# 29 products of zeros in place of 23 ahead of the first transposes

## The chip, the cores and the metric

The kernel runs on one core of one Trainium2 chip. The metric is device time in microseconds (us) of one execution. The kernel before has a median of 334.01 us over three executions (333.19 to 335.12). Engines are named as the profile names them: PE (TensorE, matrix products; PEld its weight loads), DVE (VectorE), ACT (ScalarE), POOL (GpSimd) and SP (SyncE, here a queue for transfers).

## The reference

Two layers follow each other. The first is attention with a band of 32 positions to either side and 8 global positions, for 8 batches of 8 heads, 576 positions and 64 dimensions. The second takes the 4608 tokens of 512 values through two dense products with a softplus between them.

```
mask = |pos_i - pos_j| <= 32, or i global, or j global
attn = softmax(where(mask, q @ k.T / 8, -1e9));  x = attn @ v
out  = softplus(x @ w_in) @ w_out        # 512 -> 2048 -> 512
```

## The kernel before, in words

The attention is done in blocks of 32 queries. A group of four blocks (a pair n in the code) has its scores s of 8 heads in two PSUM banks; a score product has a form of 32x128, one block of queries against four blocks of keys (previous, own, next, global). DVE takes row maxima m, ACT the exponentials st, DVE or POOL normalises them to pn, DVE transposes them to pt, and PE multiplies by v into xo. For the first two batches q and k are turned on PE: transposes tr against an identity, and beside them small products pick that choose the global rows. The output xo is cast to xT, and the dense layer follows in eight or nine phases: products h (xT by w_in, L1288), softplus to g on ACT, products o (g by w_out, L1299).

The first four groups have the mask added on PE, by a product of the identity with a mask tile (s, L1062 and L1072). L1062 waits for the mask tile, which DVE writes last in L641. The value products of the first phase are opened ahead by four products of zeros into xo (L1239), one for each of its PSUM banks; the real ones are L1253.

The order of the instructions on every engine is made before the run by a planner (class `_Order`). It goes through a fixed table of jobs (`ORDER`) and gives each job a planned time, from costs per operation in nanoseconds and a model of when PE's instructions arrive in blocks of 256. Each tile of PSUM gets, in that planned time, the bank that comes free first.

Where the planner sees PE without work for at least 700 ns in the first 34,000 ns (`WARM`), `keep` puts in a group of products of zeros: `fill_in` multiplies a cleared part of a spare v tile (vb) by itself, 128x128 by 128x512, into a free bank (tile warm, L731). Nothing reads the results. Before, their number is the planned gap times `FILL` (0.55) over `FILLT` (220 ns), rounded down. The first gap starts at PE's planned start of 1200 ns and ends at the planned start of L1062. Each group is also counted in the model of instruction blocks (`self.issued`), and takes a bank from then on.

Of the kernel before, what the change touches and what calls it, by code (L numbers as in the profile page):

```python
# [20 lines left out]
class _Order:  # L21
# [131 lines left out]

    WARM = 0
    FILL, FILLT, NARROW, NFILL, NFILLT = 0.55, 220, 0, 0.8, 140
    STARVE = 900
    fill = None

    def keep(self, t0, t1, order):

        if self.fill is None or t1 > self.WARM or t1 - t0 < 700:
            return
        free = [(self.closed(k), n) for n, k in enumerate(self.banks)]
        free = [x for x in free if x[0] is not None and x[0] <= t0 + 300]
        if not free:
            return
        n = min(free)[1]
        thin = t0 < self.NARROW
        share, step = (self.NFILL, self.NFILLT) if thin else (self.FILL, self.FILLT)
        count = int((t1 - t0) * share / step)  # L170
        key = ("warm", len(order))
        j = dict(cost={"PE": (0, 0)}, emit=lambda e: self.fill(key, count, thin), at=t0, end=t0 + count * step, on="PE", n=-1, deps=[])
        self.fetch = self.stall(t0, count * step, 2 * count)[1]
        self.issued += 2 * count
        self.users[key] = [j]
        self.banks[n] = key
        self.bank[key] = n
        order.append(j)
# [26 lines left out]
    def run(self, free):  # L205
# [16 lines left out]
        while ready:  # L222
# [6 lines left out]
            for j in self.picked(ready):  # L229
# [6 lines left out]
                for e in j["cost"] if not self.given else [self.given[0][1]]:  # L236
# [7 lines left out]
                    elif e == "DVE" and j["port"]:  # L244
                        if self.other[0] <= t + 100 and self.other[1] > t:
                            t = self.other[1] + self.STARVE
                    elif e == "POOL" and t < self.mine[1]:
                        t = self.mine[1] + (self.STARVE if t < self.mine[0] else 0)
                    if self.TABLE and j["table"] and j["table"] != table:
# [1222 lines left out]
```

## Time and profile before

| what | value |
|---|---|
| median of three executions | 334.01 us (333.19 to 335.12) |
| profiled execution | 333.27 us, of which 331.2 us are the span from the first to the last instruction |
| mean granted TensorE clock | 0.979 |
| products of zeros (warm, L731) | 41, busy 13.9 us |
| products h and o | 768, busy 138.2 us, and 592, busy 138.3 us |

The page divides the span by engine; the chain of waits follows the end of the program back to what released each step; the timeline lists instructions in order of time, with the idle time before them in brackets and what ended it. Views by stretch give the busy time of each engine and the clock that was granted to TensorE, as a share of full speed. A span shorter than the time of the execution is normal: some microseconds lie before the first and after the last instruction.

### The profile page before, as it was taken

Reading aid. Unit: us, or ns where it says so; the run is one execution under the profiler, and the core shown is the slowest. Engines: PE = TensorE matmul, PEld = TensorE weight load, DVE = VectorE, ACT = ScalarE, POOL = GpSimd, SP = SyncE. Lnnn points to the kernel's source line nnn. Section 1 sums busy time; section 2 is a strip of 40 time slices with the busy share of each in tenths; the row PEclk is TensorE's granted clock in tenths of the full one; section 3 lists DMA queues with packets and bytes.
Section 4 is the critical chain, followed back from the end, with each engine's and each line's share of the span. In section 5 each row is a group of like instructions: output and inputs, shape, how many; then the busy total and the mean of one; then the engine's idle time right before and its main releaser. Section 6 shows DMA issues by size and latency. Waiting matters only on the chain.

```text
span 331.2 us, 12091 instructions
## 1 busy us (share of the span) xinstructions
PE 322.2 (97%) x5285; PEld 172.5 (52%) x5285; DVE 220.2 (66%) x386; ACT 234.1 (71%) x459; POOL 196.0 (59%) x175
## 2 busy tenths in 40 slices
PE   8797999999999999999999999999999999999996
PEld 3455886565555445544455445444544454454444
DVE  7587588856997799894895985278785970431000
ACT  5579879686698896388648867996749746915622
POOL 7825908996786568859579396829183927240000
PEclk9767999999999999999999999999999999999999
DMA  7997898989898999999989980370010011001002
GB/s 193 187 204 187 186 185 144 150 141 212 174 162 147 175 215 143 202 206 200 181 164 185 152 189 2 115 158 3 4 65 0 36 65 70 27 34 63 34 32 96
DMA packets 168796, 42.14 MB, mean 127 GB/s; under 512 B 153256, under 2 KB 165800, under 8 KB 168744
## 3 DMA queue, kind: packets, MB, share of 16 engines
q1 hardware_dynamic: 155928, 27.15, 46.3%
q0 software_dynamic: 10944, 11.08, 16.5%
q10 hardware_dynamic: 1872, 3.15, 2.5%
q8 instruction: 41, 0.67, 0.9%
q14 instruction: 11, 0.09, 0.1%
HBM read 36.71 MB, written 9.44 MB: 139 GB/s over the span
## 4 chain that ended last, share of the span: by engine, by line
PE 92%; DVE 3%; ACT 2%; DMA 1%; issue 1%; DVEq 0%
PE o L1299 38%; PE h L1288 38%; PE xo L1253 5%; PE s L1079 4%; PE ov L999 2%; PE tr L859 1%; PE pick L888 1%; PE warm L731 1%; DMA gi<-in_global_idx_dram 1%; ACT st L1115 1%; PE sg L970 1%; PE pick L901 1%; PE s L1062 0%; DVE qx L722 0%; ACT qx L722 0%
## 5 line engine op out<-in xcount | busy, mean ns | idle before, releaser
L1299 PE MATMUL o<-wout,g 128*128 128x512 bf16 (+1 forms) x592 | 138.3, 374 | 0.0
L1288 PE MATMUL h<-xT,win 128*128 128x512 bf16 (+3 forms) x768 | 138.2, 328 | 0.0
L1294 ACT ACTIVATE g<-h 128x512 bf16<-128x512 f32 (+3 forms) x192 | 84.5, 504 | 29.9 <-PE h L1288 26.7
L1134 POOL TENSOR_TENSOR pn<-st,rs 128x1024 bf16<-128x1024 f32 (+1 forms) x38 | 66.9, 1769 | 58.1 <-DVE rs L1128 52.9
L1288 PEld LDWEIGHTS <-win 128*128 128x128 bf16 x768 | 67.6, 99 | 59.8 <-issue 1.1
L1299 PEld LDWEIGHTS <-g 128*128 128x128 bf16 x592 | 55.9, 98 | 60.7 <-ACT g L1294 1.0
L1102 POOL TENSOR_TENSOR st<-st,m 128x1024 f32<-128x1024 f32 x32 | 60.2, 1893 | 27.7 <-DVE m L1096 27.7
L1083 DVE TENSOR_TENSOR st<-s,mask 128x512 f32<-128x512 f32 x64 | 41.1, 676 | 18.5 <-PE s L1079 18.4
L1126 DVE TENSOR_REDUCE sm<-st 128x8 f32<-128x1024 f32 x32 | 38.5, 1203 | 14.9 <-ACT st L1119 14.7
L1096 DVE TENSOR_REDUCE m<-st 128x8 f32<-128x1024 f32 x32 | 37.9, 1208 | 0.3
L722 ACT COPY osb<-o 128x512 f32<-128x512 f32 (+1 forms) x30 | 17.2, 577 | 22.6 <-PE o L1299 20.2
L1119 ACT ACTIVATE st<-st 128x1024 f32<-128x1024 f32 x32 | 32.7, 1053 | 0.3
L1143 DVE STREAM_TRANSPOSE pt<-pn 128x512 int32<-128x512 int32 x36 | 24.5, 689 | 5.2 <-POOL pn L1134 5.1
L722 ACT CAST xT<-xo 128x512 bf16<-128x512 f32 (+3 forms) x28 | 11.7, 467 | 18.4 <-PE xo L1253 18.4
L722 DVE CAST xT<-xo 128x512 bf16<-128x512 f32 (+3 forms) x20 | 11.3, 600 | 18.6 <-PE xo L1253 18.6
L1294 ACT ACT_TABLE_LOAD x15 | 19.2, 1283 | 1.7 <-PE h L1288 1.5
L1119 ACT ACT_TABLE_LOAD x14 | 18.0, 1283 | 0.7 <-ACT osb L722 0.4
L719 POOL TENSOR_SCALAR qb<-stage 128x1152 bf16<-128x1152 f32 (+2 forms) x15 | 16.8, 1126 | 1.7 <-DMA stage<-in_q_dram 1.1
L1079 PEld LDWEIGHTS <-qx 64*32 64x32 bf16 x1152 | 10.4, 92 | 9.5 <-issue 6.3
L722 POOL CAST vb<-stage 128x1152 bf16<-128x1152 f32 x12 | 13.7, 1145 | 2.7 <-DMA stage<-in_v_dram 2.7
L731 PE MATMUL warm<-vb 128*128 128x512 bf16 x41 | 13.9, 485 | 1.3 <-DVE vb L553 1.3
L1079 PE MATMUL s<-kx,qx 64*32 64x128 bf16 x1152 | 14.6, 225 | 0.2
(127 smaller groups left out, 291.4 us busy)
## 6 DMA issues: line engine op xcount, KB each, us to landing
stage<-in_v_dram SPq DMA_DIRECT2D x56, 144.0 KB, 4.3
stage<-in_q_dram SPq DMA_DIRECT2D x48, 144.0 KB, 3.9
stage<-in_k_dram SPq DMA_DIRECT2D x48, 144.0 KB, 4.3
out_dram<-osb POOLq DMA_DIRECT2D x24, 256.0 KB, 3.2
out_dram<-osb ACTq DMA_DIRECT2D x11, 256.0 KB, 2.0
stage<-in_q_dram SPq DMA_DIRECT2D x4, 512.0 KB, 5.9
stage<-in_k_dram SPq DMA_DIRECT2D x4, 512.0 KB, 7.1
win<-in_moe_w_in_dram POOLq DMA_DIRECT2D x8, 256.0 KB, 7.4
```

The lines of the kernel that those rows point to most:

```text
L722: {"ACT": nc.scalar.copy, "DVE": V.tensor_copy, "POOL": nc.gpsimd.tensor_copy}[e](out, in_)
L1079: nc.tensor.matmul(out=PS["s", n, g][quad(a), x, :], lhsT=qx[b % 2][rows(g), a, j * BL:(j + 1) * BL], rhs=kx[b % 2][rows(g), a, e0 * BL:(e ...
L1083: V.tensor_tensor(out=PS["st", n][:, h, :, :], in0=PS["s", n, h][:, :, :], in1=mask[:, h, j0:j0 + PB, :, :].rearrange("p j s i -> p j (s i ...
L1096: V.reduce_max(out=m[:], in_=flat(PS["st", n], h0, h1), axis=AX)
L1102: on(e).tensor_tensor(out=t, in0=t, in1=over(PS["m", n, y][:], SL * BL), op=OP.subtract)
L1119: nc.scalar.activation(out=t, in_=t, func=AF.Exp)
L1126: V.reduce_sum(out=sm[:], in_=flat(PS["st", n], h0, h1), axis=AX)
L1134: on(e).tensor_tensor(out=PS["pn", n][:, :, :, h0:h1].rearrange("p x s h -> p h x s"), in0=PS["st", n][:, h0:h1], in1=PS["rs", n, y][:].re ...
L1143: V.transpose(out=bass.AP(base.tensor, base.offset, ap=[list(base.ap[0]), [2 * STEP, PB // 2], [STEP + BL // 2, 2], [1, SL * BL]]), in_=PS ...
L1288: nc.tensor.matmul(out=h[:, :], lhsT=w_in_t[c // 4][:, kd, c % 4 * P:(c % 4 + 1) * P], rhs=PS["xT", m][:, kd, lo:hi], start=(kd == 0), sto ...
L1294: nc.scalar.activation(out=PS["g", m, c][:, lo:hi], in_=PS[key][:, lo_of(c, hi - lo)], func=AF.Softplus)
L1299: nc.tensor.matmul(out=PS["o", m, ns, a][:, :], lhsT=PS["g", m, kf][:, ns * P:(ns + 1) * P], rhs=w_out_t[kf // 4][:, kf % 4, a:z], start=( ...
```

## The change

`keep` counts differently where the gap starts before 5400 ns of planned time (`COLD`). It takes 0.93 of the gap (`LONG`) in place of 0.55, and counts the part ahead of 5400 ns at 427 ns a product (`COLDT`), the rest at 220 ns. Only the first group starts that early. All other costs, the table of jobs and the other groups' rule stay.

```
+    COLD, COLDT, LONG = 5400, 427, 0.93
...
         share, step = (self.NFILL, self.NFILLT) if thin else (self.FILL, self.FILLT)
         count = int((t1 - t0) * share / step)
+        if t0 < self.COLD:
+            span = (t1 - t0) * self.LONG
+            cold = min(span, self.COLD - t0)
+            count = int(cold / self.COLDT + (span - cold) / step)
+            step = span / count
```

The order on DVE, ACT, POOL and SP is the same as before. On PE three places differ. The new code is six lines longer, so a line above 172 of before has a number higher by six after (L1062 is L1068, L1079 is L1085, L1239 is L1245, L1253 is L1259, L1288 is L1294, L731 is L737).

The first place is the end of the first group, ahead of the mask product. Rows of before (46 to 53):

```order
L731 MATMUL warm<-vb_67 128x512
L1062 LDWEIGHTS ident [waits DVE_49]
L1062 MATMUL s<-mask,ident 128x512 [waits Pool_49]
L1062 LDWEIGHTS ident [waits Activation_49]
L1062 MATMUL s<-mask,ident 128x512 [waits Pool_49]
L859 LDWEIGHTS kb [waits Activation_49]
L859 MATMUL tr<-ident,kb 128x128
```

and of the change (58 to 64):

```order
L737 MATMUL warm<-vb_67 128x512
L1068 LDWEIGHTS ident [waits DVE_49]
L1068 MATMUL s<-mask,ident 128x512 [waits Pool_49]
L1068 LDWEIGHTS ident [waits Activation_49]
L1068 MATMUL s<-mask,ident 128x512 [waits Pool_49]
L865 LDWEIGHTS kb [waits Activation_49]
L865 MATMUL tr<-ident,kb 128x128
```

The group ahead of these rows has 29 products in place of 23, so everything behind stands 12 rows later (a weight load and a product each).

The second place is PE between the last scores of the fourth group and the first value products. A wait names the engine that is waited for. Rows of before (691 to 706):

```order
L1079 LDWEIGHTS qx_68
L1079 MATMUL s<-kx_70,qx_68 32x128
L731 LDWEIGHTS vb_67
L731 MATMUL warm<-vb_67 128x512 [waits Activation_49]
...
L1239 LDWEIGHTS vb_67
L1239 MATMUL xo<-vb_67 128x128 [waits PE_49]
...
L1239 LDWEIGHTS vb_67 [waits DVE_49]
L1239 MATMUL xo<-vb_67 128x128 [waits Activation_49]
L1239 LDWEIGHTS vb_67
L1239 MATMUL xo<-vb_67 128x128 [waits Activation_49]
L1253 LDWEIGHTS vb_66
L1253 MATMUL xo<-pt,vb_66 64x64 [waits DVE_49]
```

and of the change (703 to 714):

```order
L1085 LDWEIGHTS qx_68
L1085 MATMUL s<-kx_70,qx_68 32x128
L1245 LDWEIGHTS vb_67
L1245 MATMUL xo<-vb_67 128x128 [waits Activation_49]
L1245 LDWEIGHTS vb_67
L1245 MATMUL xo<-vb_67 128x128 [waits PE_49]
...
L1245 LDWEIGHTS vb_67 [waits DVE_49]
L1245 MATMUL xo<-vb_67 128x128 [waits Activation_49]
L1259 LDWEIGHTS vb_66
L1259 MATMUL xo<-pt,vb_66 64x64 [waits DVE_49]
```

The two products of zeros are gone. Row 703 was the weight load of the fourth L1239; now it is the weight load of the last score product, and the four L1239 stand at 705 to 712. With that group gone, xo and most later tiles of PSUM (323 of 365) have another bank than before.

The third place is PE behind the first 60 products of h. Rows of before (923 to 932):

```order
L1288 LDWEIGHTS win_127
L1288 MATMUL h<-xT,win_127 128x128
L731 LDWEIGHTS vb_67
L731 MATMUL warm<-vb_67 128x512
L731 LDWEIGHTS vb_67
L731 MATMUL warm<-vb_67 128x512
L731 LDWEIGHTS vb_67
L731 MATMUL warm<-vb_67 128x512
L1253 LDWEIGHTS vg_74
L1253 MATMUL xo<-pt,vg_74 64x256 [waits DVE_49]
```

and of the change (931 to 938):

```order
L1294 LDWEIGHTS win_127
L1294 MATMUL h<-xT,win_127 128x128
L737 LDWEIGHTS vb_67
L737 MATMUL warm<-vb_67 128x512
L737 LDWEIGHTS vb_67
L737 MATMUL warm<-vb_67 128x512
L1259 LDWEIGHTS vg_74
L1259 MATMUL xo<-pt,vg_74 64x256 [waits DVE_49]
```

Three products of zeros have become two. In all PE has 10,578 rows in place of 10,572, and 44 products of zeros in place of 41.

## The prediction

> **What bounds the kernel now.** I read the page's shares first, then the chain of waits, then the start of the timeline, since the change acts there.
>
> ```profile
> span 331.2 us, 12091 instructions
> PE 322.2 (97%) x5285; PEld 172.5 (52%) x5285; DVE 220.2 (66%) x386; ACT 234.1 (71%) x459; POOL 196.0 (59%) x175
> PE 92%; DVE 3%; ACT 2%; DMA 1%; issue 1%; DVEq 0%
> ```
>
> TensorE sets the end: 92% of the chain that ended last is PE. A microsecond won at the start reaches the end only if it lies on that chain. The timeline (start, length, engine, line, count, idle time before it) shows the stretch that the change fills:
>
> ```profile
> 1.26 6.91 PE L731 MATMUL warm<-vb 128*128 128x512 bf16 x23 [1.26 <-DVE vb L553]
> 4.65 0.15 PEld L731 LDWEIGHTS <-vb 128*128 128x128 bf16 x1 [0.28 <-issue]
> 4.99 2.69 PEld L731 LDWEIGHTS <-vb 128*128 128x128 bf16 x13 [0.18 <-issue]
> 10.24 0.60 PE L1062 MATMUL s<-mask,ident 128*128 128x512 bf16 x2 [2.07 <-DVE mask L641]
> ```
>
> The 23 products of zeros run from 1.26 to 8.17; then PE idles for 2.07 us, until VectorE has written the mask that L1062 reads. No product of zeros touches that VectorE work.
>
> The granted clock over stretches of 3.41 us, cut where it steps (columns: stretch, length, PE busy and count, clock, DMA share, GB/s):
>
> ```profile
> 4.88:8.30 3.42, 3.29 (x15) 1.00 1.18 294
> 8.30:11.71 3.41, 1.47 (x26) 1.00 1.53 225
> 11.71:15.12 3.41, 2.94 (x40) 0.50 2.16 147
> 15.12:18.54 3.42, 3.42 (x81) 0.50 1.46 201
> 18.54:21.95 3.41, 3.41 (x51) 0.50 1.22 201
> 21.95:25.36 3.41, 3.41 (x113) 1.00 1.24 205
> 25.36:28.78 3.42, 1.58 (x63) 1.00 0.63 138
> 28.78:32.19 3.41, 3.41 (x70) 0.50 0.98 262
> ```
>
> All steps lie on one grid of 3.41 us. Two stretches with PE busy for under half (1.47 and 1.58 us) are each followed by half clock; a full one of large products (18.54 to 21.95) brings it back. The first products also run at half pace although the column still shows 1.00: single weight loads of 0.15 us up to 4.65, 13 in 2.69 us from 4.99. So the products do their work on the clock only if they make the stretch 8.30 to 11.71 count as busy.
>
> **The change part by part.** The listings show three edits on PE and none on the other engines: 6 products more at the head, 2 fewer before the first value products (L1239), 1 fewer after the first 60 products of h.
>
> *Six more at the head.* At full clock the pitch is (2.69 - 0.10) / 12 = 0.216 us. Six take 6 x 0.216 = 1.29 us of 2.07 idle, so the last ends at 8.17 + 1.29 = 9.46, and 0.78 us of idle is left. Cost 0; cover: the VectorE mask chain. Without cover they would cost 1.29.
>
> *Two fewer before L1239.* First the timeline of that place, then the chain of waits (start, length, what), then the instruction queue (packets, MB, share).
>
> ```profile
> 25.71 0.60 PE L731 MATMUL warm<-vb 128*128 128x512 bf16 x2
> 25.94 0.37 PEld L1239 LDWEIGHTS <-vb 128*128 128x128 bf16 x3
> 28.48 0.10 PEld L1239 LDWEIGHTS <-vb 128*128 128x128 bf16 x1 [2.17 <-issue]
> 27.09 0.40 ACT L1010 ACTIVATE vg<-ov,grs 128x128 bf16<-128x128 f32 x1
> 27.05 0.71 DVE L1143 STREAM_TRANSPOSE pt<-pn 128x512 int32<-128x512 int32 x1
> 27.86 0.66 DVE L1094 TENSOR_REDUCE m<-s 128x4 f32<-128x512 f32 x1
> ```
> ```profile
> 27.28 0.22 PE xo L1239
> 27.50 0.99 issue
> 28.71 0.60 PE xo L1253 x46
> ```
> ```profile
> q8 instruction: 41, 0.67, 0.9%
> ```
>
> The two products end at 26.31 and PE waits anyway until 28.48: their removal saves nothing. But the wait is not a data wait. The fourth L1239 loads its weights only at 28.48, although its data (vg, 27.49) and those of the next rows (pt, 27.76) are there. The instruction queue moved 41 packets for 10,572 PE rows, 258 each; so I take it that row 703, where that load stands, begins a block that had not arrived. The Trainium skill (Runtime: NRT & Kernel Launch, Instruction fetch mechanics) gives 16 KiB blocks of 256 instructions; 0.67 MB in 41 packets agrees. The stall stays at row 703, and the change puts another instruction there: the last pair of scores, then four L1239. Behind the late pair wait four openings of 0.054 us (128 columns, a quarter of the 512-column pitch of 0.216), some 0.2 us. Against it, the row whose issue asks for the block comes 12 rows, six products, earlier: between 0 and 0.43 us (six of the 60 h products, 4.32 us below). Net between -0.2 and +0.2; I take +0.1, since the six rows there are scores, smaller than h's. The row maximum at 27.86 reads the other bank's scores, already written; if it waited for the late pair, it would end near 29.3, where VectorE's next step waits for xo anyway (28.71 + 0.60 = 29.31).
>
> *One fewer after h.* The VectorE row of the timeline, then the chain.
>
> ```profile
> 31.51 1.27 DVE L1143 STREAM_TRANSPOSE pt<-pn 128x512 int32<-128x512 int32 x2
> ```
> ```profile
> 29.32 0.96 PE warm L731 x2
> 30.28 4.32 PE h L1288 x60
> 34.60 0.65 PE warm L731 x3
> 35.25 1.01 PE xo L1253 x75
> ```
>
> Here the products of zeros are on the chain: the tile that xo reads (pt) was there by 32.78 (31.51 + 1.27), yet it starts behind 0.65 us of three zero products. One fewer is -0.22 us. It could be lost again at the next ScalarE wait (0), so between -0.22 and 0; I take -0.2, since the chain stays on PE behind it (xo at 35.25).
>
> *PSUM banks.* With one group of zeros gone, later tiles get other banks. The rows of before cannot show that cost; PE was idle for only 3.1 us after 40 us (291 - 287.89), so it lies between -1 and +1. I take 0: the planner picks banks by the same rule.
>
> ```profile
> 40.00:331.00 291.00, 287.89 (x4678) 150.91 (x4676) 191.03 (x305) 204.96 (x350) 169.18 (x118) 1.00 0.60 119
> ```
>
> *The clock.* In 8.30 to 11.71 PE's busy time becomes 1.47 + (9.46 - 8.30) = 2.63 of 3.41 us, 77%. Is that enough? For: only stretches under 50% were followed by a drop. Against:
>
> ```profile
> 8.30:11.71 3.41, 1.02 (x12) 1.00 1.53 225
> 15.12:18.54 3.42, 1.70 (x23) 0.50 1.46 201
> ```
>
> These are the same stretches for the transposes (tile tr) alone. 15.12 to 18.54 was 100% busy, half of it transposes, and did not lift the clock: they seem to weigh little. Without them the new stretch holds 2.63 - 1.02 = 1.61 us, 47%, hardly more than the 1.58 that lost the clock at 28.78. So I take the clock to drop at 11.71 as before. The Trainium skill (TensorE: Matmul & The Clock Gate, Part 4) says that transposes do not count as PE busy in the same way; the trace agrees, 3.42 us busy at 0.50. Its closing table asks only for no idle gaps over about 3 us; by that the 2.07 us gap would have cost nothing, which the drop at 11.71 contradicts.
>
> *Sum.* 0 + 0.1 - 0.2 + 0 + 0 = -0.1 us. Against the profiled execution's own time (333.27: span 331.2 and 2.07 around it) that is 333.17. That execution lies 0.74 under the median, near the fastest of 333.19 to 335.12; from the median 334.01 I get 333.9.
>
> **The rivals.**
>
> *The clock is kept (faster).* If 77% is enough, the next stretch runs at full clock. The chain's transposes show what it is worth, and a row of ScalarE what could follow:
>
> ```profile
> 10.85 0.22 PE tr L859 x4
> 11.07 0.08 PE pick L865 x4
> 12.89 0.45 PE tr L859 x4
> 13.33 0.09 PE pick L865 x4
> 13.96 0.89 PE warm L731 x2
> ```
> ```profile
> 21.89 1.01 ACT L982 ACTIVATE pg<-sg,gnb 128x320 bf16<-128x320 f32 x2 [1.20 <-DVE gnb L977]
> ```
>
> A set of transposes and picks takes 0.30 at full clock and 0.54 at half; three sets lose 0.7 us, and the two zero products 0.45. Part goes to VectorE's and ScalarE's copies behind them, so I put 0.5 on the chain, -0.1 - 0.5: 333.4. The stretch 11.71 to 15.12 is then itself thin (transposes and 0.43 us of zeros) and would drop the clock at 15.12. Only if it held to 21.95 would the 6.8 us there, all PE, shrink too; then ScalarE's wait of 1.20 goes as well, 1.7 in all: 332.2. Chances 0.20 and 0.06.
>
> *The products overshoot.* The grid of the clock need not start where it did here. If the clock comes up to 3.2 us later, each later microsecond moves the end of the zeros by 1 - 0.216 / 0.43 = 0.50 us (0.43 is the pitch of the single loads, 0.15 + 0.28 idle), at most to 9.46 + 1.6 = 11.06 against 10.24. The last 0.2 us drain while the next runs, which leaves +0.6, where 23 products would still end before 10.24. It decides once the clock comes more than 1.6 us later. Against: this profile has 0.78 to spare. The chain then moves by what is over, -0.1 + 0.6: 334.5. Chance 0.16. The Trainium skill (TensorE: Matmul & The Clock Gate, Part 1) calls the window free-running with a run-variable number of cold products; a single trace cannot show it.
>
> *A second drop (slower).* With two zero products gone, PE's gap of 26.31 to 28.48 begins some 0.5 us earlier. Where the grid cuts this gap in two, before could keep its clock and the change lose it: place 25.71, price up to 3.41 us at half clock in the 60 products of h, 1.7. It decides when one stretch falls under about 1.6 us busy. Here the clock drops there already, so nothing is added: 335.6, chance 0.06.
>
> **How the numbers follow.** No change of the clock has 0.52, kept for one stretch 0.20, overshoot 0.16, kept to 21.95 0.06, second drop 0.06. This measurement tells apart about 0.5%, 1.7 us: the first three lie within it, and only 332.2 and 335.6 sit at its edge. With some room for banks and scatter: faster 0.09, same 0.83, slower 0.08. The likeliest is 333.9; the range takes the kept stretch (333.4), the overshoot (334.5), a microsecond for the banks to either side and the scatter of a median: 332.8 to 335.0.
>
> **What would show it.** The head: one group of 29, L1062 still at about 10.2 with idle of about 0.8; a later start says overshoot. The clock: 0.50 from 11.7 says the six bought nothing; 1.00 until 15.1 says the window counted as busy. The block: a weight load of L1079 alone near 28.4 with idle "issue", L1239 right behind. The h group: two zeros behind it and xo some 0.2 us earlier. I am wrong if the clock stays at 1.00 through 12 to 22, or if idle time after 40 us leaves 3 us by more than one.

## The result and the profile after

The changed kernel has a median of 332.32 us against 334.41 for the kernel before beside it: a ratio of 0.994 (95% interval 0.9914 to 0.9966), 2.1 us or 0.6% faster. The prediction said 333.9, no measurable change, with a range down to 332.8: it was wrong. The profiled execution took 331.25 us, 2.02 under that of before, with a mean clock of 0.995 in place of 0.979.

The page of the changed kernel: span, shares, and the shares of the chain by engine.

```profile
span 329.2 us, 12097 instructions
PE 319.7 (97%) x5288; PEld 171.3 (52%) x5288; DVE 219.3 (67%) x386; ACT 233.9 (71%) x459; POOL 195.9 (60%) x175
PE 91%; DVE 2%; SPq 2%; DMA 2%; issue 1%; ACT 0%
```

PE bounds the kernel as before; its busy time fell by 2.5 us although it does three products more. The timeline shows what happened at the head, at row 703 and behind the first h:

```profile
1.26 8.97 PE L737 MATMUL warm<-vb 128*128 128x512 bf16 x29 [1.26 <-DVE vb L559]
10.27 0.61 PE L1068 MATMUL s<-mask,ident 128*128 128x512 bf16 x2
...
26.42 0.23 PE L1085 MATMUL s<-kx,qx 64*32 64x128 bf16 x1 [3.02 <-issue]
26.58 0.40 PE L1245 MATMUL xo<-vb 128*128 128x128 bf16 x4
26.90 0.57 PE L1259 MATMUL xo<-pt,vb 32*64 32x64 bf16 x40
...
28.39 4.45 PE L1294 MATMUL h<-xT,win 128*128 128x128 bf16 x60
32.67 0.59 PE L737 MATMUL warm<-vb 128*128 128x512 bf16 x2
33.20 0.44 PE L1259 MATMUL xo<-pt,vg 32*64 32x256 bf16 x8
```

The zeros end at 10.23 and L1068 starts at 10.27, with no idle time ahead of it and hardly later than before (10.24). The last pair of scores stands alone at row 703 and waits 3.02 us for its block. The first h starts at 28.39 (30.07 before), the second stretch of xo at 33.20 (35.18). That is 1.98 us, and the span is 2.0 shorter: all of it was won ahead of 33 us. The windows show where:

```profile
9.85:13.26 3.41, 2.96 (x53) 2.28 (x52) 1.61 (x4) 1.22 (x2) 2.77 (x5) 1.00 1.90 163
13.26:16.67 3.41, 3.02 (x90) 2.01 (x86) 3.04 (x7) 3.05 (x9) 2.92 (x5) 1.00 2.18 167
...
23.50:26.91 3.41, 0.49 (x7) 0.32 (x8) 2.60 (x9) 3.03 (x17) 1.30 (x2) 1.00 0.96 159
26.91:30.32 3.41, 3.41 (x71) 2.69 (x70) 1.54 (x5) 2.63 (x16) 2.74 (x3) 0.50 0.88 250
...
40.00:329.00 289.00, 285.80 (x4598) 149.18 (x4595) 190.70 (x303) 202.95 (x344) 168.66 (x117) 1.00 0.62 119
```

The clock stays at 1.00 until 26.91, where the kernel before had lost it at 11.71 for three stretches. It goes only behind the stretch that holds the wait for row 703. After 40 us PE idles for 3.2 us (3.1 before).

One thing warns against reading the gain off these two traces: the grid of the clock lies elsewhere. Here the clock first came up at 6.43, in the trace of before at 4.88. So the two kernels were not seen under the same conditions. The means over executions in what follows leave out four executions of 410 to 805 us, of three kernels (the one before among them).

### The profile page after: what moved, and what is told of

It is laid out like the page before. It is cut to its first block, busy times and chain, and to the rows that moved or that the text cites. A ratio compares the mean times of both kernels' runs of the same rounds, so it can differ in the third digit from the quotient of the medians.

```text
span 329.2 us, 12097 instructions
## 1 busy us (share of the span) xinstructions
PE 319.7 (97%) x5288; PEld 171.3 (52%) x5288; DVE 219.3 (67%) x386; ACT 233.9 (71%) x459; POOL 195.9 (60%) x175
## 4 chain that ended last, share of the span: by engine, by line
PE 91%; DVE 2%; SPq 2%; DMA 2%; issue 1%; ACT 0%
PE o L1305 39%; PE h L1294 38%; PE xo L1259 5%; PE s L1085 4%; DMA stage<-in_q_dram 2%; PE ov L1005 2%; SPq L522 1%; PE pick L894 1%; SPq L526 1%; PE sg L976 1%; DVE qx L728 1%; PE tr L865 1%; PE warm L737 1%; PE pick L907 1%; DVE pick L601 0%
## 5 line engine op out<-in xcount | busy, mean ns | idle before, releaser
L1294 PE MATMUL h<-xT,win 128*128 128x512 bf16 (+3 forms) x768 | 137.9, 328 | 0.1
L1294 PEld LDWEIGHTS <-win 128*128 128x128 bf16 x768 | 67.7, 99 | 59.5 <-issue 0.8
L1085 PE MATMUL s<-kx,qx 64*32 64x128 bf16 x1152 | 14.5, 220 | 4.0 <-issue 3.0
L1085 PEld LDWEIGHTS <-qx 64*32 64x32 bf16 x1152 | 10.4, 90 | 12.6 <-issue 9.1
L1317 POOL DMA_DIRECT2D out_dram<-osb x24 | 13.7, 573 | 2.9 <-ACT osb L728 1.4
L737 PE MATMUL warm<-vb 128*128 128x512 bf16 x44 | 13.7, 461 | 1.3 <-DVE vb L559 1.3
```

What stands on the lines that cost most here:

```text
L1085: nc.tensor.matmul(out=PS["s", n, g][quad(a), x, :], lhsT=qx[b % 2][rows(g), a, j * BL:(j + 1) * BL], rhs=kx[b % 2][rows(g), a, e0 * BL:(e ...
L1294: nc.tensor.matmul(out=h[:, :], lhsT=w_in_t[c // 4][:, kd, c % 4 * P:(c % 4 + 1) * P], rhs=PS["xT", m][:, kd, lo:hi], start=(kd == 0), sto ...
```

## The experiments

Eighteen runs were made beside the kernel before, in five sets on four chips; some repeat a kernel. Single executions of one kernel scatter by about 1.3 us, so I give the mean over all executions of a kernel with its standard error, beside the ratio of its own comparison. The edits change what is emitted and not what the planner counts, so the rest of the order stays that of the kernel that is edited. "Narrow" is a product of zeros 8 columns wide: it takes two rows on PE and next to no busy time, its result isn't read, and where the head has one, it stands behind the wide ones. "Rows" is by how much PE's rows behind 60 products of h are moved against the kernel before.

| kernel | head | later zeros | rows | mean, us | executions | ratio |
|---|---|---|---|---|---|---|
| before (all runs, with e1) | 23 wide | before | 0 | 334.05 +- 0.1 | 187 | e1: 1.0019 |
| e3, i2 | 23 wide | change | -6 | 333.7 +- 0.3 | 24 | 1.0007, 0.9969 |
| i1 | 26 wide | change | 0 | 333.4 +- 0.5 | 12 | 0.9967 |
| h1 | 23 + 3 narrow | before | +6 | 333.4 +- 0.5 | 12 | 0.9981 |
| g1 | 23 + 6 narrow | before | +12 | 333.3 +- 0.4 | 12 | 1.0002 |
| h4 | 23 + 9 narrow | before | +18 | 333.6 +- 0.4 | 10 | 0.9999 |
| e2 | 29 wide | before | +12 | 333.0 +- 0.4 | 11 | 0.9967 |
| e4 | 23 + 6 of 128 columns | change | +6 | 332.8 +- 0.3 | 12 | 0.9968 |
| f4 | 23 + 6 narrow | change | +6 | 332.8 +- 0.35 | 12 | 0.9969 |
| f2 | 12 + 17 of 128 columns | change | +6 | 333.45 +- 0.2 | 12 | 0.9978 |
| change (with f1, h2) | 29 wide | change | +6 | 332.3 +- 0.15 | 44 | 0.994, 0.9943, 0.9957 |
| f3 | 35 wide | change | +18 | 333.7 +- 0.6 | 12 | 0.9971 |
| g3, h3 | 28 + 7 narrow | change | +18 | 331.8 +- 0.3 | 24 | 0.9938, 0.9952 |
| g4 | 26 + 23 narrow | change | +46 | 337.8 +- 0.6 | 6 | 1.014 |
| g2 | 23 wide; 6 narrow at row 1668 | before | 0, then +12 | 335.4 +- 0.3 | 12 | 1.0061 |

### The parts of the change, and the unchanged kernel (e1 to e4)

e1 is the kernel before as it is. e2 adds six products to its head; e3 is the change without them; e4 is the change with the six 128 columns wide in place of 512.

```
e2  emit=... self.fill(key, count + (6 if t0 < 5400 else 0), thin)          # in the kernel before
e3  emit=... self.fill(key, count - (6 if t0 < self.COLD else 0), thin)     # in the change
e4  matmul(out=ps[:, 0:P if small else 4 * P], ...)   with small = x >= n - 6 at the head
```

> The kernel before, unchanged, so that each of its executions has its granted clock listed. Theory A (the six products keep the clock): nearly all executions show a mean clock near 0.979, as in the profile of before, and the time is that of before, ratio 1.000. Rival C (the grid of the clock differs from execution to execution, and before keeps its clock in part of them): the clocks lie in two groups, near 0.98 and 0.995, and the fast group is about 2 us faster.

> The six more products at the head alone; the two groups further on and the PSUM banks as before. Theory A: clock near 0.995 and nearly the whole gain, -1.6 to -2.0 us (the third zero product behind h is still there, 0.2 us). Rival B (the gain comes from the removed groups and the other PSUM banks): no gain, within 0.4 us of before.

> The change without the six products: 23 at the head, the two groups further on and the banks as in the change. Theory A: clock near 0.979, time within 0.4 us of before. Rival B: most of the gain, -1.6 us or more.

> The change, with the six added products 128 columns wide in place of 512: the same rows, banks and blocks of instructions, but only 6 x 0.054 = 0.32 us more busy time at the head in place of 1.29. Theory A: the clock drops again in most executions (near 0.98) and the time is within 0.5 us of before. Rival B': the gain comes from the shifted rows (the block of instructions is asked for 12 rows earlier): it stays at -1.6 us or more whatever the clock.

The unchanged kernel gave 1.0019 (0.9986 to 1.0052). Its mean clocks run from 0.979 to 1.000, where theory A expected nearly all of them near 0.979, and its trace upset the reading of the first one. The windows of e1, the clock's stretches:

```profile
9.33:12.74 3.41, 2.04 (x37) 1.74 (x38) 1.55 (x5) 1.75 (x3) 2.75 (x6) 1.00 1.83 182
12.74:16.16 3.42, 3.08 (x89) 2.07 (x87) 3.21 (x7) 2.57 (x6) 3.11 (x6) 1.00 2.29 157
...
43.47:46.88 3.41, 1.86 (x88) 1.44 (x86) 1.36 (x3) 0.64 (x3) 0.00 (x0) 1.00 1.20 199
46.88:50.29 3.41, 3.41 (x33) 2.82 (x31) 3.37 (x8) 1.92 (x5) 0.00 (x0) 0.50 1.07 192
```

In this execution the clock came up at 5.92, and 23 products were enough to keep it: the second xo began at 32.82, earlier than in the trace of the change. Yet the execution took 335.46 us. The chain of e1 shows why:

```profile
37.27 1.57 issue
38.84 1.05 PE h L1288 x8
...
44.03 1.55 issue
45.58 0.22 PE pick L869 x4
```

PE stands still twice for 1.5 us, in the middle of h and of picks. Counted over the weight loads and products of the trace, the rows that wait are 1211 and 1467. They are 256 apart, and within four rows of 1215 and 1471, where the second and the third block behind the one of row 703 begin if every block has 256 rows. By the trace's records of the instruction queue these blocks landed at 37.55 and 44.25, and PE went on 1.28 and 1.33 us later. The second wait also cost the clock from 46.88 to 50.29.

e2 gave 0.9967 (0.993 to 1.0004), e3 1.0007 (0.9975 to 1.004), e4 0.9968 (0.9936 to 1.0). So the six products carry more of the gain than the removed ones; but e2's 1.1 us are less than theory A expected, and six thin products give 1.1 us as well, which neither theory expected. Either thin products keep the clock as well, or it counts that PE's rows move.

### Wide, thin and narrow (f1 to f4)

f1 is the change. f2 has 12 wide products and 17 of 128 columns; f3 has 35 wide; f4 has 23 wide and six narrow.

```
f2  small = x >= n - 17, 128 columns      f4  small = x >= n - 6, 8 columns      # both 29 products
f3  emit=... self.fill(key, count + (6 if t0 < self.COLD else 0), thin)
```

> The change itself, beside the other three, on the same chip. Theory A (the products keep the clock at the head): mean clock 0.993 to 0.995 in at least 8 of 10 executions, -1.5 to -2.2 us against before. If the earlier -2.0 was scatter: nearer to -1.

> The change with only 12 of the 29 products 512 columns wide and 17 of 128 columns: same rows, banks and blocks, but the head's work ends at about 6.6 us and PE then idles some 3.6 us. Theory A: the clock is lost at the head in nearly every execution (mean clock 0.99 or lower, two or more stretches at half), and the time is that of before or up to 1 us over it. Rival B' (what counts is the 12 rows by which the instruction blocks shift): -1.2 us or more, as with six thin products.

> The change with 35 products at the head, all else as in the change: they end at 10.7 to 11.6 us, behind the mask (10.2). Theory A with overshoot: clock kept as in the change, but L1068 starts 0.5 to 1.4 us late; time between the change and +1 us over it. If nothing but the clock counts: as the change. Rival B': 12 more rows earlier, a further -0.5 us or more.

> The change with the six added products 8 columns wide: rows, banks and blocks of the change, but no busy time added (6 x 8 columns). Theory A: clock and time as in the run with 23 at the head, within 0.6 us of before. Rival B': as with six products of 128 columns, -1.2 us or more.

The change again gave 0.9943 (0.9917 to 0.997). Six narrow products, with hardly any busy time, keep more than half of it: 0.9969 (0.9937 to 1.0001). f2 gave 0.9978 (0.9951 to 1.0004). By these ratios both lie between what the two theories expected. The head of f2 is thin, and its windows show the clock lost:

```profile
8.16:11.57 3.41, 1.35 (x24) 1.12 (x25) 1.86 (x8) 1.62 (x4) 3.41 (x6) 1.00 1.53 233
11.57:14.98 3.41, 2.94 (x38) 2.10 (x37) 2.61 (x5) 1.67 (x3) 2.45 (x6) 0.50 2.15 147
```
```profile
14.98:18.40 3.42, 3.42 (x79) 0.50 1.51 201
```

(The last line has PE alone: busy time, clock, DMA share, GB/s.) With the same rows as the change, f2 is 1.2 +- 0.25 us slower: that is what the clock is worth between a kernel that hardly ever keeps all of it (a mean clock of 0.990 or less in 11 of 12 executions) and one that mostly does. And though f2 loses the clock oftener than the kernel before, it is no slower. Something other than the clock gains here. f3 is the overshoot, 0.9971 (0.993 to 1.0012); its timeline:

```profile
1.26 9.57 PE L737 MATMUL warm<-vb 128*128 128x512 bf16 x35 [1.26 <-DVE vb L559]
10.66 0.59 PE L1068 MATMUL s<-mask,ident 128*128 128x512 bf16 x2
```

L1068 starts 0.4 us late, and most of the gain is gone (333.7 +- 0.6 against 332.3). The 0.4 us do not account for all of that: f3 also has 12 rows more than the change, and its trace waits 0.97 and 1.63 us for the blocks of rows 1211 and 1723.

### Rows alone, early and late (g1 to g4)

g1 puts six narrow products at the head of the kernel before; g2 puts them at row 1668 of it, ahead of products o; g3 and g4 put narrow ones at the head of the change.

```
g1  self.fill(key, count + 6, 6) at the head          # 23 wide, 6 narrow
g2  for x in range(6 if (m, ns) == (0, 2) else 0):
        matmul(out=PS["o", m, ns, a][:, 0:8], lhsT=ident[:, :], rhs=ident[:, 0:8], ...)
g3  28 wide, 7 narrow          g4  26 wide, 23 narrow
```

> The kernel before with six products 8 columns wide behind its 23 at the head: every later row of PE moves back by 12, no busy time is added, and both removed fills stay. Theory R (rows: the gain comes from where the 256-row instruction blocks fall, so that those needed at about 37 and 44 us come in time) expects nearly the whole of what the six 8-wide products gave on the change's side: 1.0 to 1.3 us under the kernel before, ratio 0.996 to 0.997. Theory C (clock: the six products gain by keeping PE busy in the stretch ahead of the transposes) expects the time of the kernel before, ratio 0.999 to 1.001.

> The kernel before with six products 8 columns wide in row 1668 and those behind it, ahead of the first products of an output tile: the same 12 rows more in all, but behind the rows (1216 and 1472) at which the blocks of 37 and 44 us begin, so these fall as before. Theory R expects no gain: 0 to +0.3 us, ratio 1.000 to 1.001. Theory C expects the same 0. If this gains 1 us as well, it isn't the blocks of 37 and 44 us but a later one, or the total.

> The change with seven products 8 columns wide in place of the last of its 29 at the head: 12 rows more than the change, the same busy time. Theory R has no fixed sign here: the blocks at 37 and 44 us are asked for earlier again, others fall elsewhere: between -0.5 and +0.5 us against the change, so 0.993 to 0.996 of the kernel before. Theory C expects the time of the change, 0.994.

> The change with 26 wide products and 23 of 8 columns at the head: 40 rows more than the change, busy time less by 3 wide products. The block that begins at row 703 then begins 40 rows earlier in the work, where the late pair of scores no longer stands. Theory R: the wait at row 703 keeps its end or shortens by up to 1 us, and blocks 3 and 4 come earlier still: -1.0 to +0.5 us against the change, 0.991 to 0.996. Theory C: 0 to +0.3 against the change, 0.994 to 0.995.

g1 gave 1.0002 (0.997 to 1.0035): no gain in its own comparison, 0.8 +- 0.4 us over all executions of before. Theory R had promised 1.0 to 1.3. g2, from which both theories expected nothing, lost: 1.0061 (1.003 to 1.0092), or 1.3 us over all executions of before. g3 gave 0.9938 (0.9908 to 0.9969), a mean of 331.3 and so 1.0 us under the change, more than either theory expected; it was run again as h3. The timeline of g2 has a wait on the block behind the added rows (row 1723 by the trace):

```profile
51.49 1.03 PE L1301 MATMUL o<-wout,g 128*128 128x512 bf16 x4 [1.37 <-issue]
```

That this wait is what g2 lost is not shown: its trace also waits 1.1 us at row 1467, ahead of the added rows, and five traces of other kernels wait 0.8 to 1.6 us at row 1723 (e2, f2, f3, f4, h2).

g4 gave 1.014 (1.0096 to 1.0184), 5.5 us over the change, and missed both expectations by far. Its second xo began at 30.97, earlier than in any other trace, and the clock held from 5.03 to 172.28. The loss is far from the head. The timeline of g4:

```profile
171.57 0.21 PE L1085 MATMUL s<-kx,qx 64*32 64x128 bf16 x1 [2.69 <-issue]
...
237.97 2.12 PE L1305 MATMUL o<-wout,g 128*128 128x512 bf16 x9 [1.36 <-issue]
```

and its windows:

```profile
168.86:172.28 3.42, 0.57 (x10) 0.31 (x4) 2.82 (x5) 1.32 (x3) 2.67 (x3) 1.00 0.97 194
172.28:175.70 3.42, 3.42 (x10) 1.22 (x8) 3.09 (x4) 0.00 (x0) 3.42 (x3) 0.50 0.78 124
```

These waits stand at rows 6585 and 8631: 19 and 27 blocks behind row 1723, less 2 and 4. The blocks landed at 170.26 and 236.47, 1.46 and 1.49 us before PE went on. Together they are 4.05 us, and the first also cost the clock for a stretch. Over all twenty traces, every gap of PE's weight loads above 0.6 us after 34 us, 18 of them in eleven traces, stands at the start of such a block. So the rows count, by several microseconds, through the blocks; but which way a shift goes can't be told from the row numbers.

### Rows again, and the fastest version again (h1 to h4)

h1 and h4 are g1 with 3 and 9 narrow products; h2 is the change, h3 is g3.

> The kernel before with three products 8 columns wide behind its 23: all later rows 6 further back, as the rows of the change stand from its third group of zeros on, and no busy time added. If rows alone carry most of the gain (theory R): 0.8 to 1.2 us under the kernel before, ratio 0.9965 to 0.9975. If the clock carries it (theory C): the time of the kernel before, 0.999 to 1.001.

> The change itself, unedited: both theories expect what it gave twice, a ratio of 0.994 to 0.995 (1.7 to 2.0 us under the kernel before).

> The change with 28 wide and 7 narrow products at the head, again. It gave 0.9938 and a mean of 331.26 us against 332.3 for the change. If its 12 rows more are worth something: 0.5 to 1.1 us under the change in this same run. If that was scatter: within 0.4 us of the change.

> The kernel before with nine products 8 columns wide behind its 23: all later rows 18 further back, as in the version with 28 wide and 7 narrow products from its third group of zeros on. Theory R: as fast as rows alone can make it, 1.0 to 1.8 us under the kernel before, 0.9945 to 0.997. Theory C: 0.999 to 1.001.

h1 0.9981 (0.9941 to 1.002), h4 0.9999 (0.9961 to 1.0036): each alone shows nothing. h1, g1 and h4 together have a mean of 333.4 +- 0.25, so rows alone give 0.65 +- 0.3 us, under what theory R expected and, at little more than twice its error, over nothing. The change gave 0.9957 (0.9924 to 0.999). The version with 28 wide and 7 narrow gave 0.9952 (0.9913 to 0.9992), level with the change in the same set: that it beats the change isn't shown (over both runs 0.5 +- 0.3 us).

### The clock with the rows of before (i1, i2)

i1 is the change with 26 products at the head; i2 is e3 again.

> The change with 26 products at the head, three fewer than it has: from its third group of zeros on every row has the number it has in the kernel before (10,572 rows in all), and the head is busy for three products longer than before, half of what the change adds. Theory C (what counts is that PE is busy long enough to keep the clock): most of the gain, 332.3 to 333.0 us by the mean, 1.0 to 1.7 under the kernel before. Theory R (what counts is where the rows fall): the time of the change without its six, 333.7 to 334.2. Half of each: 333.2.

> The change with 23 products at the head, again: both theories expect what it gave, 0 to 0.4 us from the kernel before.

i1 gave 0.9967 (0.9934 to 1.0), a mean of 333.4 +- 0.5: between the two theories. i2 gave 0.9969 (0.9942 to 0.9995), 1.0 us where 0 to 0.4 was expected; with e3 it makes 0.3 +- 0.3. The traces of the two show the clock kept and lost. First the timeline and the windows of i1, in which the clock came up at 4.81:

```profile
1.26 7.52 PE L737 MATMUL warm<-vb 128*128 128x512 bf16 x26 [1.26 <-DVE vb L559]
10.21 0.60 PE L1068 MATMUL s<-mask,ident 128*128 128x512 bf16 x2 [1.43 <-DVE mask L647]
```
```profile
8.22:11.63 3.41, 1.98 (x29) 1.25 (x28) 1.80 (x8) 1.64 (x4) 3.41 (x6) 1.00 1.55 233
11.63:15.05 3.42, 2.88 (x76) 1.98 (x78) 2.88 (x5) 2.30 (x6) 2.47 (x6) 1.00 2.29 146
...
25.29:28.70 3.41, 2.01 (x54) 1.10 (x55) 1.68 (x7) 2.00 (x13) 3.23 (x4) 0.50 0.56 116
28.70:32.12 3.42, 3.42 (x35) 3.42 (x33) 1.73 (x6) 3.40 (x16) 2.16 (x3) 0.50 1.13 293
```

then the timeline and the windows of i2, at 4.30:

```profile
1.26 6.62 PE L737 MATMUL warm<-vb 128*128 128x512 bf16 x23 [1.26 <-DVE vb L559]
10.30 0.60 PE L1068 MATMUL s<-mask,ident 128*128 128x512 bf16 x2 [2.42 <-DVE mask L647]
```
```profile
7.71:11.13 3.42, 1.00 (x13) 0.60 (x13) 2.26 (x9) 1.99 (x4) 3.42 (x6) 1.00 1.47 251
11.13:14.54 3.41, 3.21 (x46) 2.76 (x42) 2.13 (x4) 1.13 (x2) 2.44 (x6) 0.50 2.18 146
```

1.98 us of busy time kept the clock (8.22 to 11.63 of i1), 1.00 did not (7.71 to 11.13 of i2). But i1 pays at the other end: with its grid the wait for row 703 is followed by two stretches at half clock, 25.29 to 32.12.

All twenty traces, by where the clock first came up (us) and whether the stretch ahead of the transposes kept it:

| head | kept | lost |
|---|---|---|
| up to 23 wide | 5.92 (e1), 6.97 (g1), 7.07 (f4), 7.26 (h4) | 4.04 (g2), 4.30 (i2), 4.49 (e3), 4.75 (f2), 4.88 (before), 5.30 (e4), 5.53 (h1) |
| 26 to 35 wide | 4.00 (h2), 4.81 (i1), 4.96 (e2), 5.01 (f3), 5.03 (g4), 5.76 (h3), 6.25 (f1), 6.43 (change), 6.47 (g3) | none |

With 23, the place of the grid decides; with 26 and more the clock was kept in all nine traces, with rises from 4.00 to 6.47. The mean clock of the executions says the same: it was 0.985 or less in 65 of 273 with 23 wide products or fewer, and in 1 of 109 with 26 to 35.

## Why the prediction was wrong, point by point

**The head: right.** The six zeros run while PE waits for the mask, and cost nothing: L1068 starts at 10.27 against 10.24. The prediction had them end at 9.46 with the clock up at 4.88, and 0.50 us later for each microsecond that it comes later. At 6.43 that is 9.46 + 0.78 = 10.24; the trace has 10.23. The overshoot rival's mechanism is real too, as f3 shows with 0.4 us of it. In the change it bites little: at the latest rise seen, 7.26, the same rule gives 10.65, 0.4 us over.

**Row 703: right in place.** The late pair stands there alone, and xo follows 0.48 us later, where before took 0.16 from the restart (28.48) to xo (28.64): +0.3 by the rows in place of +0.2. The wait became longer, 3.02 us, only because all ahead of it came sooner.

**One fewer after h, and the banks: right within the error.** The trace has two zeros and 0.43 us on the chain in place of 0.65. With the banks, the removed products are worth 0.3 +- 0.3 us (e3, i2 against before, with 6 rows fewer) or 0.6 +- 0.3 (e4, f4 against h1, g1, h4); the prediction had 0.1 for both edits.

**The clock: the step that failed.** "I take the clock to drop at 11.71 as before" was wrong twice. First, the measure. The prediction worked out 2.63 us busy for that stretch, took off 1.02 us of transposes, and kept 1.61 us, 47%. Both the taking off and its reason fail.

The records of products overlap on PE, so their times can't be taken from each other. In the same stretch of before, the picks alone and the mask products alone (tile s) were busy for

```profile
8.30:11.71 3.41, 0.64 (x12) 1.00 1.53 225
8.30:11.71 3.41, 0.60 (x2) 1.00 1.53 225
```

together 1.24 us, where 1.47 - 1.02 = 0.45 was left to them. With the 1.16 us of new zeros the stretch held 2.40 us, 70%, even without its transposes. The change shows the clock kept with 2.96 us in its stretch at 9.85.

The reason was that 15.12 to 18.54, full and half of it transposes, did not lift the clock. Two later traces lifted it out of such a stretch: f2 out of 14.98 to 18.40 above, as full and with as much time in transposes (1.70 us), and i2 out of 11.13 to 14.54, with 3.21 us busy, of which the transposes alone are

```profile
11.13:14.54 3.41, 2.69 (x20) 0.50 2.18 146
```

The picks and the zeros of that stretch come to 1.55 + 0.49 = 2.04 us at most, while 3.00 us without any transposes (e2, 25.45 to 28.86) did not lift the clock. So the single stretch of before did not show that transposes weigh little; why it failed to lift the clock where f2's did is open. For keeping the clock, e1 has the clearest stretch: 9.33 to 12.74 kept it with 2.04 us, of which the transposes, the picks and the mask products alone are

```profile
9.33:12.74 3.41, 1.52 (x19) 1.00 1.83 182
9.33:12.74 3.41, 0.98 (x16) 1.00 1.83 182
9.33:12.74 3.41, 0.60 (x2) 1.00 1.83 182
```

Without the transposes at most 0.98 + 0.60 = 1.58 us would count. That is no more than the 1.58 of before, without transposes, that lost the clock at 28.78. So they seem to count for keeping it; this rests on one stretch. The Trainium skill (TensorE: Matmul & The Clock Gate, Part 4) says that transposes do not count as PE busy in the same way, and the prediction leaned on that; the stretches of i2 and e1 disagree.

Where the bound lies is read from the windows of h2

```profile
24.49:27.90 3.41, 1.98 (x60) 1.24 (x61) 2.38 (x8) 2.69 (x17) 2.50 (x3) 1.00 0.72 123
27.90:31.31 3.41, 3.41 (x35) 3.41 (x33) 2.12 (x7) 3.39 (x16) 2.86 (x4) 0.50 1.13 302
```

of g4

```profile
23.51:26.92 3.41, 2.01 (x76) 1.26 (x77) 3.15 (x12) 3.41 (x22) 1.22 (x2) 1.00 0.97 161
```

and of e1 (PE alone), where the clock stayed up behind it until 46.88:

```profile
36.64:40.05 3.41, 1.84 (x46) 1.00 0.95 136
```

2.01 us kept the clock in g4 and 1.84 in e1; 1.98 lost it in h2 and kept it in i1, and 1.86 lost it in e1 at 46.88. Over all twenty traces, up to 8 us before their ends, every stretch at full clock with 2.0 us busy or more was followed by full clock, every one with less than 1.8 by half clock, and those between by either (some traces lack 45 of some 5,285 products, so single figures can be a little low). The predicted 2.63 lies well above. The Trainium skill (TensorE: Matmul & The Clock Gate, Why this matters for your kernels) asks only for no idle gaps over about 3 us; i2 lost the clock behind a gap of 2.42, so that rule is too lenient here, as the prediction held.

Second, the single trace. The prediction took the drop at 11.71 as a property of the kernel before, where it is one of the grid: in four of eleven traces with 23 wide products or fewer the clock was kept. The Trainium skill (TensorE: Matmul & The Clock Gate, Part 1) says that the window is "free-running"; the traces agree, with first rises from 4.00 to 7.26, more than the +-500 ns that it names. The prediction used this for the overshoot alone.

That also sizes the term. Were the grid to fall evenly over its 3.41 us, 23 products would lose the clock for rises from about 4.0 to 5.7, half of the executions. Where they lose it, about 1 us goes (1.2 between f2 and the change; of the executions of before, 40 with a mean clock of 0.985 or less took 334.0 +- 0.2 us and 58 with 0.993 to 0.995 took 333.0 +- 0.1), so by this estimate 0.5 on average. Measured by the mean: the change against e4 and f4, which have its rows, 0.5 +- 0.3; e2 against h1, g1 and h4 0.4 +- 0.5; i1 against e3 and i2 0.3 +- 0.5. The rival "kept for one stretch" had priced it at 0.5, with a chance of 0.20. The rival "kept to 21.95" had named 332.2, almost the result, and the pair of profiled executions, 2.0 us apart, looks like it: the clock held past 21.95, and ScalarE's wait of 1.20 fell to 0.40. But these two executions are extremes of the clock, one with four stretches at half clock and one with one. Over all executions the clock is worth about 0.5 us, because the kernel before keeps it too in part of them.

**What no term held: the other blocks.** The prediction followed the block at 703 and none behind it, because PE idled for only 3.1 us after 40 us in that execution. In others the next blocks come late. The mean clocks of before show how much lies there: the 67 executions at 0.988 to 0.990 are its slowest (334.9 +- 0.1 us), not the 40 at 0.985 or less. e1's trace is one of these 67, and its time went at the blocks. Moving the rows by 6 to 18 gives 0.65 +- 0.3 us (h1, g1, h4 against before), and moving them by 12 gives 0.95 +- 0.35 (e4, f4 against e3, i2). So of 1.8 us by the means, some 0.8 come from the rows, some 0.5 from the clock, some 0.45 from the removed products and the banks, each with an error of 0.2 to 0.3. Taken against the kernel before of each set alone, the same three parts are some 0.7, 0.7 and 0.6 of 1.95 us.

**What stays open.** That rows matter is shown: f4 and g2 add hardly anything else, and g4 stands still at the starts of blocks. That the change's own 0.8 us come from the blocks behind 703 fits, but is not shown. In traces with the rows of before or 6 fewer at these blocks, four of six have a wait above 0.6 us at the block of 1211 or 1467; with 6 to 18 more, two of thirteen. One of these two is h1, whose rows at these blocks are the change's own, with waits of 1.8 and 1.9 us in a long execution. At the next block, of 1723, it is the other way round: none of the five with 0 or -6 waits there, and five of the thirteen do, h2 (the change) with 1.1 us among them (g2, with 12 rows more there, waits 1.5). So part of the waits only moves to a later block, and the row numbers don't decide alone. What goes with a wait is when the block lands. I count from PE's row some 318 ahead, a mark that I chose, since no trace shows which row asks for a block. In all twenty traces the block of 1211 lands 2.5 to 4.75 us after that where PE waits less than 0.6 us there, and 4.8 to 6.5 after in the five others (e1, e3, f3, g4, h1). The mean is 4.9 us over the six traces with 0 or -6, and 3.9 over the thirteen with +6 to +18. Meanwhile loads fill the DMA engines; the windows of e1, where it took 6.3 us (the DMA share is the last but one),

```profile
33.00:35.00 2.00, 2.00 (x115) 1.97 (x112) 0.85 (x2) 1.44 (x8) 1.57 (x6) 1.00 0.96 260
35.00:37.00 2.00, 2.00 (x30) 1.83 (x27) 1.54 (x3) 1.72 (x7) 1.97 (x6) 1.00 0.99 254
```

and of the change, where it took 3.5:

```profile
33.00:35.00 2.00, 2.00 (x107) 1.76 (x106) 1.17 (x3) 1.72 (x10) 1.12 (x2) 1.00 0.87 248
35.00:37.00 2.00, 2.00 (x35) 1.87 (x33) 1.17 (x2) 1.72 (x8) 1.86 (x8) 1.00 0.76 215
```

That the block waits behind such a load is argued from this; which one, and what of it the edit decides, was not tried.

## What to carry to other kernels

One profile shows one place of the clock's grid: before a stretch is called lost or kept, look at other executions, and fill an idle stretch so far that it is kept wherever the grid lies, here to more than 2 of 3.41 us busy. Times of overlapping records can't be subtracted: look at what is left, not at what is taken off. Here an edit that added or removed rows of PE moved the block starts behind it, and won or lost more than the edit itself (5.5 us in g4); so compare an edit with a version that has the same rows, here with narrow products. Where single executions scatter by 1.3 us, parts of half a microsecond need dozens of executions each, and even then only their sum is sure.

## What was not expected of the hardware

- The clock's grid of 3.41 us lies anywhere against the program: first rises from 4.00 to 7.26 us in twenty traces. One stretch at half clock lowers the mean clock by 0.005.
- In the 18 waits at block starts after 34 us, PE went on 1.2 to 1.6 us after the block had landed. PE stands still there for up to 3 us, deep in the kernel too (2.69 us at 169 us in g4). The Trainium skill (Runtime: NRT & Kernel Launch, Instruction fetch mechanics) calls the cost of crossing a block "mostly hidden"; for most of the 41 blocks it is, in these traces not for all.
- Six products 8 columns wide, which compute nothing, made one kernel 1.0 us faster (f4 and e4 against e3 and i2) and another 1.3 us slower (g2).
- In this kernel's records transposes ran at the granted clock: a set of four takes 0.22 us of the chain at full clock and 0.45 at half in the trace of before.
